# An early job of 272 places, the rest of its expert with the tokens held stationary, and GpSimd's last work shared with VectorE

## The chip, the cores and the metric

The kernel runs on one core of a Trainium2 chip. The metric is the device time of one execution in microseconds (us). Three runs of the kernel before took 909.02, 901.28 and 900.65 us; their median is 901.28 us. The profiled execution, from which every duration below comes, took 895.38 us, and its recorded span is 893.5 us, so 1.9 us lie outside the span and the median lies 5.9 us above it.

## The reference

The inputs are q, k and v with 8 batches, 8 heads, 576 positions and 64 features, and the weights of a mixture of 8 experts. Cut to what matters:

```python
scores = scale * q @ k.T
thresh = scores.max(-1) - tau
attn   = exp(where(scores >= thresh, scores, -1e9) - scores.max(-1))
attn   = attn / (attn.sum(-1) + 1e-9)
x      = (attn @ v)                      # to 4608 tokens x 512
skip   = x @ w_skip > 0                  # only these are computed
e      = argmax(x @ w_gate);  g = its softmax weight
out    = x + g * (relu(x @ w1[e]) @ w2[e])   # 512 -> 1024 -> 512; others pass
```

With the inputs that are drawn, the eight experts get 393, 350, 336, 298, 275, 263, 237 and 197 tokens (worked out from the reference on a host). 357 of the 393 are known before the last five 128-token tiles are through the gate.

## The kernel before, in words

**Precision.** Products of the mixture are made of three products each: a float32 operand is split into a high part that TensorE's fp32r type holds and a low part (the difference), and high·high, low·high and high·low are summed. In the attention the weights `p` are split into float16 parts in the same way, `phh`/`tph` (high, L540 on ScalarE or L542 on VectorE) and `phl`/`tpl` (low, L1009, on GpSimd only); `ph..` is of 128 rows x 1152 and `tp..` the remaining 64 positions of two heads.

**The attention stage.** It is a list of operations, 32 pairs of heads (8 batches x 4). Each pair has scores for the maximum (L824 on TensorE, L829 on VectorE), transposed scores (L797), the exponential (L967, ScalarE), the threshold mask (L972, VectorE, gives `p`), the split, the product with the values (L1037, L1040, L1041, called AV below), and the normalised rows `xb` (L1091) and `x` (L1104) on GpSimd. Rows go to `out` in DRAM; logits come from their transposes (L1147, L1173). For every two batches a gate on VectorE (L1252 to L1411) works out the expert, the gate weight and a place in that expert's list, and GpSimd writes (token, gate) there by indirect DMA, 128 tokens at a time (L1395, `lst<-rec,si`). The last two batches do that in two portions, of four and of five tiles. A planner (class `Plan`, with `SEEDS` for perturbed trials and `OFF` for offsets) simulates the list with a table of costs and so sets the order on every engine.

**The early job.** When all but the last five tiles are in the lists, the expert with most tokens is picked (L1443), and 256 of its tokens become the first job, still inside the plan: the list is loaded, ids are made (L1498, L1499, VectorE), rows are gathered (L529, GpSimd), transposed (L1570), and put through layer 1 (L1603 on TensorE; L1617 and L1620 finish it), whose weights were split on L1541.

**The jobs behind it.** They are in program order: rows are gathered (L1822, issued at L529), transposed and split (`prep_x`, L1832 to L1841), then layer 1 (L1845; products at L1857) and layer 2. Layer 2 either holds blocks of up to 128 tokens of `h` stationary and streams 512 columns of w2 (L1881, products at L1891: 24 for each block), or, where the number of places is no multiple of 128 and at most 320 and the job is not the last, holds w2 stationary, streams the places (L1898, products at L1910: 96) and transposes back. Layer 1 always is 96 products of as many columns as there are places. Weights of the next job are split meanwhile (`split_w`, L1817 ScalarE high, L1818 VectorE or GpSimd low). Jobs: early 256; the rest of that expert, 256; then 384, 352, 320, 288, 288, 256, 256. A loop behind them (L2081) takes tokens beyond these places, one pass for each surplus block, and does not run with these inputs.

## Time and profile before

| what | before |
| --- | --- |
| median of three runs | 901.28 us |
| profiled execution / its span | 895.38 / 893.5 us |
| TensorE busy | 859.5 us (96%) |
| attention stage and early layer 1 | 0 to 640.3 us |
| layer 2 of the early job, then the rest of its expert | 641.9 to 682.2 us |
| seven jobs | 682.2 to 887.8 us |
| last store and end | 887.8 to 893.5 us |

A window's row gives the start and end of a stretch, its length, and for each engine the busy us and, in brackets, the number of instructions; then the mean granted clock of TensorE as a share of 2.4 GHz, the busy share of the DMA engines and GB/s. A timeline's row gives the start, the time that a run of like instructions covers, and in square brackets how long the engine sat idle just before, and what ended that.

### The profile page before, as it was taken

The numbers are of one execution on the slowest core, as the hardware profiler recorded it, in microseconds if no ns is written. First come the engines' busy times: TensorE is split into PE (matmuls) and PEld (weight loads), VectorE is DVE, ScalarE is ACT, GpSimd is POOL, SyncE is SP. The second block draws the span as 40 slices with busy tenths as digits, with TensorE's granted clock in tenths as the row PEclk, the third lists the DMA queues.
The fourth block names the chain that finished last, engine by engine and source line by source line (L and its number), as shares of the span: only waits on it lengthen the run. The fifth ranks groups of instructions, "written<-read, shape, count | busy, mean of one in ns | idle before, by whom it ended". The sixth has DMA issues, their size and how long they took to land. (4 is left out here: it accounts for less than half of the span.)

```text
span 893.5 us, 24884 instructions
## 1 busy us (share of the span) xinstructions
PE 859.5 (96%) x9745; PEld 802.5 (90%) x9745; DVE 682.8 (76%) x1605; ACT 607.5 (68%) x923; POOL 666.6 (75%) x461
## 2 busy tenths in 40 slices
PE   9999999999999999999999999989989999999997
PEld 6888999999999999998889998978879898999986
DVE  6888888988997878999888899894535554476782
ACT  1768988798988798888789878786314452454451
POOL 5576998799789798999899979999336455473463
PEclk9999999999999999999999999999999999999999
DMA  7996778569577767857865864523156635544540
GB/s 174 250 217 164 179 168 235 145 157 254 136 154 203 186 149 200 210 130 188 187 145 136 238 150 97 141 99 120 60 164 232 212 97 184 189 146 162 189 139 19
DMA packets 77422, 147.58 MB, mean 165 GB/s; under 512 B 28178, under 2 KB 28178, under 8 KB 77304
## 3 DMA queue, kind: packets, MB, share of 16 engines
q1 hardware_dynamic: 72616, 136.33, 57.9%
q0 software_dynamic: 4544, 9.65, 3.2%
q8 instruction: 77, 1.26, 0.6%
q14 instruction: 41, 0.34, 0.1%
q10 hardware_dynamic: 144, 0.00, 0.0%
HBM read 68.68 MB, written 15.21 MB: 94 GB/s over the span
## 5 line engine op out<-in xcount | busy, mean ns | idle before, releaser
L1009 POOL TENSOR_TENSOR phl<-p,phh 128x1152 f16<-128x1152 f32 x128 | 305.3, 2394 | 36.3 <-ACT phh L540 14.4
L829 DVE TENSOR_REDUCE mx<-banks 128x1 f32<-128x288 f32 x558 | 230.4, 448 | 27.6 <-PE banks L824 25.4
L972 DVE SCALAR_TENSOR_TENSOR p<-banks,e 128x576 f32<-128x576 f32 x288 | 214.3, 752 | 42.4 <-ACT e L967 38.2
L967 ACT ACTIVATE e<-banks,ntau 128x576 f32<-128x576 f32 x288 | 207.8, 739 | 49.8 <-PE banks L797 37.9
L824 PE MATMUL banks<-QK 128*128 128x288 f32 x1024 | 192.2, 306 | 6.5 <-DMA QK<-hl 4.1
L797 PE MATMUL banks<-QK 128*128 128x288 f32 x1024 | 183.6, 307 | 4.7 <-DVE p L972 2.9
L824 PEld LDWEIGHTS banks<-QK 128*128 128x128 f32 x1024 | 148.8, 188 | 11.5 <-DVE p L972 4.2
L797 PEld LDWEIGHTS banks<-QK 128*128 128x128 f32 x1024 | 145.9, 190 | 10.8 <-DVE p L972 6.3
L540 ACT ACTIVATE phh<-p 128x1152 f16<-128x1152 f32 x117 | 136.1, 1165 | 17.4 <-DVE p L972 10.8
L1037 PE MATMUL banks<-Vh,phh 128*128 128x65 f16 x1280 | 131.0, 195 | 0.4 <-ACT xf L540 0.4
L1041 PE MATMUL banks<-Vh,phl 128*128 128x65 f16 x1280 | 129.1, 194 | 1.1 <-POOL phl L1009 0.9
L1040 PE MATMUL banks<-Vl,phh 128*128 128x64 f16 x1280 | 129.9, 193 | 0.0
L1037 PEld LDWEIGHTS <-phh 128*128 128x128 f16 x1280 | 116.5, 98 | 7.1
L1041 PEld LDWEIGHTS <-phl 128*128 128x128 f16 x1280 | 117.3, 97 | 1.8 <-POOL phl L1009 1.7
L1040 PEld LDWEIGHTS <-phh 128*128 128x128 f16 x1280 | 117.5, 99 | 0.5 <-issue 0.4
L1818 POOL TENSOR_TENSOR wl<-wr,wh 128x1024 fp32r<-128x1024 f32 x28 | 72.5, 2606 | 33.5 <-ACT wh L1817 25.7
L1857 PE MATMUL hps<-xh,wl 128*128 128x256 f32 (+4 forms) x256 | 76.7, 300 | 0.0
L599 POOL TENSOR_TENSOR hl<-raw,hl 128x576 fp32r<-128x576 f32 x43 | 61.6, 1439 | 20.0 <-DVE hl L599 13.0
L1857 PE MATMUL hps<-xh,wh 128*128 128x256 f32 (+4 forms) x248 | 75.9, 306 | 0.0
L1857 PE MATMUL hps<-xl,wh 128*128 128x256 f32 (+4 forms) x248 | 74.8, 302 | 0.0
L1869 POOL DMA_INDIRECT out<-o,ids x21 | 21.1, 1004 | 71.9 <-DVE o L1868 29.2
L1858 ACT ACTIVATE QK<-hps 128x256 fp32r<-128x256 f32 (+4 forms) x64 | 26.9, 421 | 67.8 <-PE hps L1857 67.1
(251 smaller groups left out, 1882.1 us busy)
## 6 DMA issues: line engine op xcount, KB each, us to landing
QK<-hl SPq DMA_DIRECT2D x192, 288.0 KB
wr<-in_w SPq DMA_DIRECT2D x31, 1024.0 KB
raw<-in_qk SPq DMA_DIRECT2D x32, 576.0 KB
vraw<-in_vl SPq DMA_DIRECT2D x32, 320.0 KB
out<-xb SPq DMA_DIRECT2D x32, 256.0 KB
BD<-hl SPq DMA_DIRECT2D x64, 64.0 KB
QK<-QK SPq DMA_DIRECT2D x32, 76.5 KB
out<-x SPq DMA_DIRECT2D x8, 128.0 KB
```

The lines of the kernel that those rows point to most:

```text
L540: nc.scalar.activation(dst, src, AF.Copy)
L797: nc.tensor.matmul(ps[:, j, 0:HS], w_, x_[:, js], start=(i == 0), stop=(i == len(mm) - 1))
L824: nc.tensor.matmul(ps[:, 0:HS], w_, x_[:, js], start=(q == 0), stop=(q == len(mm) - 1))
L829: nc.vector.tensor_reduce(T["mx", g][:, o, j : j + 1], T.pop(("S", g, i, j))[:, 0:HS], AX.X, ALU.max)
L967: nc.scalar.activation(e, T["W", g, i][:, :, 0:HS], AF.Exp, bias=ntau, scale=0.125)
L972: nc.vector.scalar_tensor_tensor(T[z][:, kt % 2].rearrange("p (a b) -> p a b", a=2), T.pop(("W", g, i))[:, :, 0:HS], 0.0, T.pop(("e", g, i ...
L1009: nc.gpsimd.tensor_tensor(T["pl", g, i], T.pop(z)[:, 0:nk], T["ph", g, i], op=ALU.subtract)
L1037: nc.tensor.matmul(pv[:, c, :], x, Vh[:, vh, kt, :], start=(j + q + c == 0), stop=False, skip_group_check=True)
L1040: nc.tensor.matmul(pv[:, c, 0:D], x, Vl[:, vh, kt, :], start=False, stop=False, skip_group_check=True)
L1041: nc.tensor.matmul(pv[:, c, :], y, Vh[:, vh, kt, :], start=False, stop=(c == NM), skip_group_check=True)
L1818: lo[q % 2].tensor_tensor(w[1][:, sl], rs, w[0][:, sl].bitcast(F32), op=ALU.subtract)
L1857: nc.tensor.matmul(hp_[:, 0:cap], w_, x, start=(i == 0), stop=(i == len(mm) - 1))
```

## The change

Constants: the early job has 272 places (`CAPE`) in three blocks of 128, 128 and 16; the rest of its expert is a job `j1` of 128 places (`REST`); the seven jobs have 356, 344, 304, 280, 268, 256 and 204 places. The planner gets another list of 37 seeds (41 before), so the order of the whole attention stage is another one.

For the last two pairs, `shared()` lets the planner put `phl`/`tpl` and `xb`/`x` on VectorE as well as GpSimd.

The last 128 tokens of the picked expert lie partly in the last five tiles. Their ids and gates no longer come from the list: for each of the five tiles VectorE makes a 128x128 selection matrix (`pick_`), TensorE multiplies it with the tile's (gate, token) columns (`sum_`, 2 columns), and the result is added to what the list held before (`recb`, loaded with the early list by two more DMAs). Eight small operations (`q1` to `q5`) make the offsets.

The early job's layer 1 is made one 128-row piece of `h` at a time, all of it behind the last logits; its layer 2 is the transposed form, with the products in an order that takes low weight parts late. Beside it the next expert's w1 is split and `j1`'s rows are prepared. `j1`'s layer 1 (`layer1_s`) holds its tokens stationary and streams 512 columns of w1 (24 products), then transposes `h` back (8 transposes). The lists of the other experts are loaded behind the issue of the next expert's w1.

```diff
-CAPE = 256
-CAPS = (512, 384, 352, 320, 288, 288, 256, 256)
+CAPE = 272
+REST = 128
+CAPS = (0, 356, 344, 304, 280, 268, 256, 204)
...
-XMID = (19, 19, 23, 23)
+XMID = (8, 12, 16, 20)
...
+    def either(e):
+        return nc.gpsimd if e == POOL else nc.vector
+
+    def shared(g, pool, dve):
+        return {POOL: pool, DVE: dve} if g >= NG - LASTS else {POOL: pool}
...
+        lo = pl.op(n + OFF["pl"], fpl, [ph], shared(g, w * 0.00208 + 0.04, w / 960 + 0.1), port=BOTH)
...
+        def pick_(t):
+            if t % 4 == 0:
+                T["sel", t // 4] = ap_.tile([P, 4, P], F32, name="xf", tag="xf", bufs=2)
+            nc.vector.tensor_scalar(
+                T["sel", t // 4][:, t % 4, :], iof, tb, G["slot"][:, t : t + 1], op0=ALU.add, op1=ALU.is_equal
+            )
+
+        def sum_(t):
+            if t == 0:
+                T["rows1"] = g_tile()[:, 0, 0:2]
+            nc.tensor.matmul(
+                T["rows1"], T["sel", t // 4][:, t % 4, :], G["rec"][:, t, 1:3], start=(t == 0), stop=(t == nt - 1)
+            )
+
+        def ids_():
+            nc.vector.tensor_tensor(id1, T["rows1"][:, 1:2], recb[:, 0:1], op=ALU.add)
+
+        def gates_():
+            nc.vector.tensor_tensor(rec1[:, 0, 1:2], T["rows1"][:, 0:1], recb[:, 1:2], op=ALU.add)
...
+            nc.vector.tensor_scalar(b0, b0, float(CAPE), 1.0, op0=ALU.min, op1=ALU.add)
...
+            nc.vector.scalar_tensor_tensor(tb, pks[:, 1:2], float(NTOK), b0, op0=ALU.mult, op1=ALU.add)
...
+            mine = lstv[:, ds(early["ev"], 1), :, :].rearrange("p e c b -> p (e c) b")
+            nc.sync.dma_start(rec0, mine[:, 0:NE, :])
+            c, r = divmod(CAPE, P)
+            nc.sync.dma_start(recb[0 : P - r], mine[r:P, c, :])
+            if r:
+                nc.sync.dma_start(recb[P - r : P], mine[0:r, c + 1, :])
...
-        for f2 in range(NFT // 2):
+        for f in range(NFT):
...
-                        mm_ += [(w_h(d, fs), a), (w_h(d, fs), b_), (w_l(d, fs), a)]
...
+                        T["h0", f] = bank()[:, 0:CAPE]
+                    three = ((w_h, j.xh), (w_h, j.xl), (w_l, j.xh))
...
-                        k2 + 1 + f2 + 0.5 * i,
+                        k2 + 1 + 0.5 * f + 0.1 * i,
...
+    def plan_rest(k, j):
+        acc, ids_, gates_ = T["acc"]
+        T["id1"] = pl.op(k, ids_, acc + [T["rec0"]], {DVE: 0.12})
...
+    def list_(e):
+        nb = jobs[e + 1].nb
+        nc.sync.dma_start(recs[:, e, 0:nb, :], lstv[:, ds(evs[e], 1), 0:nb, :].rearrange("p e c b -> p (e c) b"))
...
+        def run(d, kinds):
+            if d not in yps:
+                yps[d] = ps_y.tile([P, 512], F32, name="yps", tag="yps")
+            for f in range(NFT):
+                for i in kinds:
+                    h, w_ = three[i]
+                    nc.tensor.matmul(
+                        yps[d][:, 0:cap],
+                        w_[:, f, d * P : (d + 1) * P],
+                        h[:, f, 0:cap],
+                        start=(f + i == 0),
+                        stop=(f == NFT - 1 and i == 2),
+                    )
...
+        ready = ((0, (0, 1)), (1, (0, 1)), (0, (2,)), (1, (2,))) if j is j0 else ((0, (0, 1, 2)), (1, (0, 1, 2)))
+        for d, kinds in ready + ((2, (0, 1, 2)), (3, (0, 1, 2))):
+            run(d, kinds)
...
+            for i, (x, w_) in enumerate(mm):
+                nc.tensor.matmul(hp_, x, w_, start=(i == 0), stop=(i == len(mm) - 1))
...
+            nc.scalar.activation(hs[:, fs], hp_, AF.Relu)
+        for q in range(2):
+            tp = ps_h.tile([P, 512], F32, name="hps", tag="hps")
+            for i in range(4):
+                nc.tensor.transpose(tp[:, i * P : (i + 1) * P], hs[:, (4 * q + i) * P : (4 * q + i + 1) * P], ident)
+            tv = tp.rearrange("p (f n) -> p f n", n=P)
+            hh, hl = (a[:, 4 * q : 4 * q + 4, 0 : j.cap] for a in (j.hh, j.hl))
+            nc.scalar.activation(hh, tv, AF.Copy)
...
     w2s, parts = split_w(w2v[ds(early["ev"], 1)], early["raw2"], (nc.vector, nc.vector))
...
+    w1v1 = w1v[ds(evs[1], 1)].rearrange("a p t f -> p (a t) f")
+    w1s, parts = split_w(w1v[ds(evs[1], 1)], [load_w(w1v1, i) for i in range(2)], (nc.vector, nc.vector))
+    list_(1)
+    for e in range(2, E):
+        expert_(e)
+        list_(e)
+    side = {d: [part] for d, part in enumerate(parts)}
+    side[2][:0] = [lambda d=d: prep_x(j1, d) for d in range(NDT)]
+    backs = layer2_t(j0, w2s, side)
+    gather_x(jobs[2])
+    layer1_s(j1, early["w1"], {0: backs})
     mids = {}
     for d, i in enumerate(XMID):
-        mids.setdefault((j0.nb - 1, i), []).append(lambda d=d: prep_x(jobs[1], d))
-    layer2(j0, w2s, {}, mids)
-    parts = []
+        mids.setdefault((0, i), []).append(lambda d=d: prep_x(jobs[2], d))
+    layer2(j1, w2s, {}, mids)
```

How instructions move, at three places. The first is the end of the attention stage on GpSimd. `lst<-rec,si` is a list write, `phl<-p,phh` and `tpl<-p,tph` are low parts, `xg<-out,id` is a gather of the early job's rows. Before:

```order
L1395 DMA lst<-rec,si 36864x2
L1009 TENSOR_TENSOR phl<-p,phh 128x1152
L1395 DMA lst<-rec,si 36864x2 x3
L1009 TENSOR_TENSOR tpl<-p,tph 128x576
L1009 TENSOR_TENSOR phl<-p,phh 128x1152 x2
L529 DMA xg_11841<-out,id_149 128x512 x2
L1009 TENSOR_TENSOR phl<-p,phh 128x1152
L1009 TENSOR_TENSOR tpl<-p,tph 128x576
L1009 TENSOR_TENSOR phl<-p,phh 128x1152 x3
L1091 TENSOR_TENSOR xb<-a,z 128x2x4x64
L1104 TENSOR_TENSOR x_10097<-a,z 64x128
```

With the change:

```order
L1021 TENSOR_TENSOR phl<-p,phh 128x1152
L1021 TENSOR_TENSOR tpl<-p,tph 128x576
L1103 TENSOR_TENSOR xb<-a,z 128x2x4x64
L1116 TENSOR_TENSOR x_10175<-a,z 64x128
L1452 DMA lst<-rec,si 36864x2 x12
L1103 TENSOR_TENSOR xb<-a,z 128x2x4x64
L1452 DMA lst<-rec,si 36864x2
L1021 TENSOR_TENSOR phl<-p,phh 128x1152
L1021 TENSOR_TENSOR tpl<-p,tph 128x576
L1636 TENSOR_TENSOR wl_12001<-wr,wh_11936 128x512
L535 DMA xg_12026<-out,id_149 128x512 x2
L535 DMA xg_12027<-out,id_149 16x512
```

Twelve list writes in one run and a thirteenth now stand ahead of the last `phl` on GpSimd and of the early gathers; where four `phl` stood behind the gathers, none does, and a weight split (L1636) stands ahead of them.

The second is VectorE at the same place (`p<-banks,e` is a mask, `id<-rec` makes the early ids, `wl<-` is a low part of the early w1). Before:

```order
L1541 TENSOR_TENSOR wl_11714<-raw_11453,wh_11532 128x512 x2
L972 SCALAR_TENSOR_TENSOR p<-banks,e 128x576 x2
L1083 RECIPROCAL z<-z 128x10
L972 SCALAR_TENSOR_TENSOR p<-banks,e 128x576 x3
L1498 CAST id_149<-rec_148 128x2
L1499 TENSOR_SCALAR id_149<-rec_148 128x2
L1541 TENSOR_TENSOR wl_11714<-raw_11453,w_11723 128x512 x2
L972 SCALAR_TENSOR_TENSOR p<-banks,e 128x576 x6
L1579 TENSOR_TENSOR QK_106<-banks,QK_105 128x512
```

With the change:

```order
L984 SCALAR_TENSOR_TENSOR p<-banks,e 128x576 x2
L1199 TENSOR_TENSOR lg<-lg,banks 128x64
L984 SCALAR_TENSOR_TENSOR p<-banks,e 128x576 x2
L1199 TENSOR_TENSOR lg<-lg,banks 128x64
L984 SCALAR_TENSOR_TENSOR p<-banks,e 128x576
L1589 CAST id_149<-rec_148 128x3
L1590 TENSOR_SCALAR id_149<-rec_148 128x3
L554 CAST wh_11936<-wr 128x512
L1021 TENSOR_TENSOR phl<-p,phh 128x1152
L554 CAST wh_11936<-raw_11848 128x512
L1021 TENSOR_TENSOR phl<-p,phh 128x1152
L1636 TENSOR_TENSOR wl_12001<-wr,wh_11936 128x512 x3
```

Before, six masks follow the early ids; now the ids come behind the last mask, and VectorE makes low parts `phl` there (seven of the eight of the last two pairs, with those that stand earlier).

The third is the head of the mixture, on TensorE: the end of layer 2 of the early job and what follows. Before (`yps` is layer 2, `xtp` a transpose of gathered rows; layer 1 of the rest follows, 96 products of 256 columns):

```order
L1891 MATMUL yps<-wl,QK_105 128x512 x4
L1839 MATMUL xtp<-ident,xg 128x128 x4
L1891 MATMUL yps<-wl,QK_105 128x512 x4
L1839 MATMUL xtp<-ident,xg 128x128 x4
L1857 MATMUL hps<-xh,wh_11532 128x256
```

With the change, behind the early job's 96 products of 272 columns (`hps<-w..,xh` is the stationary form of `j1`'s layer 1):

```order
L2042 MATMUL hps<-wl_12143,xh 128x512
L2042 MATMUL hps<-w_12090,xh 128x512
L2042 MATMUL hps<-w_12090,xl 128x512
L2042 MATMUL hps<-wl_12143,xh 128x512
L2049 MATMUL hps<-ident,hs 128x128 x8
L1985 MATMUL yps<-wh,QK_105 128x512
L1985 MATMUL yps<-wh,QK_106 128x512
```

The 96 products of 256 columns are gone; 24 of 512 columns and 8 transposes stand in their place, and `j1`'s layer 2 has one block of 24 products, with the transposes of the next job's rows among them. On SP's queue there, before:

```order
L1678 TENSOR_LOAD tabp
L1638 ISA
L1638 DMA recs<-lst 128x4
L1678 TENSOR_LOAD tabp
L1638 ISA
L1638 DMA recs<-lst 128x4
L525 ISA
L525 DMA wr<-in_w 128x2x1024
L525 ISA
L525 DMA wr<-in_w 128x2x1024
```

and with the change:

```order
L1774 TENSOR_LOAD tabp
L531 ISA
L531 DMA wr<-in_w 128x2x1024
L531 ISA
L531 DMA wr<-in_w 128x2x1024
L1771 ISA
L1771 DMA recs<-lst 128x6
L1774 TENSOR_LOAD tabp
L1771 ISA
L1771 DMA recs<-lst 128x6
```

The two loads of w1 now stand ahead of the seven list loads.

## Rows read from the trace of the kernel before

**Rows 1.** the page, part 1: busy us (share of span) and instructions of each engine

```profile
PE 859.5 (96%) x9745; PEld 802.5 (90%) x9745; DVE 682.8 (76%) x1605; ACT 607.5 (68%) x923; POOL 666.6 (75%) x461
```

**Rows 2.** windows: stretch, length, busy us (count) by engine, clock, DMA share, GB/s

```profile
0.00:600.00 600.00, 580.90 (x7778) 546.04 (x7778) 516.80 (x1335) 485.65 (x721) 515.06 (x366) 1.00 0.71 175
600.00:622.00 22.00, 18.90 (x294) 17.31 (x293) 13.16 (x22) 15.14 (x23) 20.97 (x13) 0.92 0.35 125
622.00:641.90 19.90, 18.28 (x171) 17.86 (x167) 7.86 (x43) 7.06 (x14) 5.80 (x8) 0.91 0.20 68
641.90:682.20 40.30, 37.34 (x211) 32.00 (x212) 19.67 (x28) 11.97 (x21) 18.71 (x14) 0.96 0.57 184
682.20:887.80 205.60, 204.11 (x1304) 189.28 (x1301) 124.55 (x180) 87.66 (x146) 105.11 (x62) 1.00 0.45 152
```

**Rows 3.** windows of L1857 alone, layer 1: 384 and 256 columns; PE, PEld, clock, DMA

```profile
682.20:699.20 17.00, 16.90 (x96) 16.60 (x96) 1.00 0.47 146
...
865.00:876.90 11.90, 11.79 (x96) 11.61 (x96) 1.00 0.11 41
```

**Rows 4.** windows of L1891 alone, layer 2: 24 products of 512 columns

```profile
699.00:704.70 5.70, 5.65 (x24) 4.34 (x24) 1.00 0.42 115
```

**Rows 5.** timeline of PE: start, length of a run, operation, count, idle before and releaser

```profile
641.91 4.04 PE L1891 MATMUL yps<-wh,QK 128*128 128x512 f32 x16 [1.63 <-ACT wh L1817]
...
655.17 1.45 PE L1839 MATMUL xtp<-ident,xg 128*128 128x128 f32 x4 [2.85 <-DMA xg<-out,ids]
```

**Rows 6.** timeline of PE, first transposes of a job and the layer 1 behind them

```profile
681.71 0.81 PE L1839 MATMUL xtp<-ident,xg 128*128 128x128 f32 x6
682.28 0.42 PE L1857 MATMUL hps<-xh,wh 128*128 128x384 f32 x1
```

**Rows 7.** timeline of PE, a transposed layer 2 that waits

```profile
799.45 0.40 PE L1910 MATMUL yps<-QK,wl 128*128 128x288 f32 x1 [1.21 <-POOL wl L1818]
```

**Rows 8.** timeline of ACT, the last of the early job and the first weights

```profile
640.32 0.60 ACT L1617 ACTIVATE QK<-banks 128x512 fp32r<-128x512 f32 x1 [0.81 <-PE banks L1603]
640.81 3.89 ACT L1817 ACTIVATE wh<-wr 128x1024 fp32r<-128x1024 f32 x4
```

**Rows 9.** timeline of DVE, the same stretch

```profile
640.95 0.69 DVE L1620 SCALAR_TENSOR_TENSOR QK<-banks,QK 128x512 fp32r<-128x512 f32 x1 [0.40 <-ACT QK L1617]
641.89 4.63 DVE L1818 TENSOR_TENSOR wl<-wr,wh 128x1024 fp32r<-128x1024 f32 x4 [0.25 <-ACT wh L1817]
```

**Rows 10.** timeline of POOL, end of the attention stage

```profile
601.22 0.97 POOL L1395 DMA_INDIRECT lst<-rec,si  x1 [0.30 <-issue]
...
608.55 1.23 POOL L529 DMA_INDIRECT xg<-out,id  x1 [0.38 <-DVE id L1499]
...
614.72 7.04 POOL L1009 TENSOR_TENSOR phl<-p,phh 128x1152 f16<-128x1152 f32 x3
```

**Rows 11.** timeline of POOL, the last five list writes

```profile
639.84 1.05 POOL L1395 DMA_INDIRECT lst<-rec,si  x1 [12.40 <-DVE si L1367]
...
644.27 1.97 POOL L1395 DMA_INDIRECT lst<-rec,si  x1 [0.30 <-issue]
646.54 0.97 POOL L1395 DMA_INDIRECT lst<-rec,si  x1 [0.30 <-issue]
```

**Rows 12.** timeline of DVE, first mask of the last pair and the early ids

```profile
602.87 0.76 DVE L972 SCALAR_TENSOR_TENSOR p<-banks,e 128x576 f32<-128x576 f32 x1 [0.15 <-ACT e L967]
...
607.10 1.11 DVE L1498 CAST id<-rec 128x2 int32<-128x2 f32 x1
```

**Rows 13.** windows of the stretches before which TensorE had waited

```profile
603.70:607.10 3.40, 3.40 (x25) 3.07 (x24) 1.44 (x3) 2.31 (x5) 3.40 (x2) 0.50 0.51 161
...
654.90:658.30 3.40, 3.03 (x9) 2.28 (x10) 0.85 (x2) 0.77 (x2) 0.30 (x1) 0.50 0.67 167
```

**Rows 14.** timeline of SP's queue, eight list loads and the next weights

```profile
648.64 6.90 SPq L1638 DMA_DIRECT2D recs<-lst  x8
655.79 1.03 SPq L525 DMA_DIRECT2D wr<-in_w  x2
```

More of the change, by code (lines that the diff above doesn't have):

```diff
@@ L61 @@
 EB = 2
+LASTS = 2
+LPE = 0.13
 PFB = 4
@@ L1379, in plan_gate @@
         w = ex
-        for f in (b1, b2, b3):
+        final = pr == B // 2 - 1 and t0 + nt == NTP
+        for f in (b1, b2, b3) + ((b1b,) if final else ()):
             w = pl.op(k + gs * 8, f, [w], {DVE: 0.12}, port=BOTH)
@@ L1430, in __init__, with x @@
             self.nb = -(-cap // P)
+            self.own = None
         def m(self, t):
             return min(P, self.cap - t * P)
+        def x(self, t):
+            return self.own[t] if self.own else self.xg[0 : self.m(t), t, :]
     j0 = Job(CAPE, rec0, id0[:, 0, :])
-    jobs = [j0] + [
-        Job(CAPS[e] - (CAPE if e == 0 else 0), recs[:, e], ids[:, e]) for e in range(E)
-    ]
+    j1 = Job(REST, rec1, id1)
+    jobs = [j0, j1] + [Job(CAPS[e], recs[:, e], ids[:, e]) for e in range(1, E)]
     def view1(w):
@@ L1504, in plan_early @@
         stored += [T["tails", bb] for bb in range(1, B - 2, 2)]
-        for t in range(CAPE // P):
+        for t in range(NE):
             def ga(t=t):
                 if t == 0:
-                    early["xg"] = cp.tile([P, CAPE // P, DM], F32, name="xg0")
-                gather(early["xg"][:, t, :], id0[:, 1, t : t + 1], NTOK - S - TL)
+                    early["xg"] = cp.tile([P, XT, DM], F32, name="xg0")
+                    last = ep.tile([P, DM], F32, name="xg2")
+                    j.own = [early["xg"][:, i, :] for i in range(XT)] + [last[0 : j.m(XT)]]
+                gather(j.own[t], id0[0 : j.m(t), 1, t : t + 1], NTOK - S - TL)
             gs.append(pl.op(k + 2, ga, [o, *stored] + [(y,) for y in gs[-1:]], {POOL: 1.04}, lat=3.0, port=()))
@@ L1558, in plan_early @@
         j.hh, j.hl = (q[:, 0:nh].rearrange("p (f n) -> p f n", n=CAPE) for q in flat)
[L1559 to L1572 removed]
+        j.xh, j.xl = (q[:, nh : nh + nx].rearrange("p (d n) -> p d n", n=CAPE) for q in flat)
@@ new lines, in plan_early, with xsl, xps @@
+        full, rest = XT * P, CAPE - XT * P
+        def xsl(q, a):
+            return q[:, 2 * a : 2 * a + 2, 0:full] if a < 2 else q[:, :, full:]
+        def xps(a):
+            n = full if a < 2 else rest
+            return T["x0", a][:, 0 : n * (2 if a < 2 else NDT)].rearrange("p (d n) -> p d n", n=n)
+        def xt(a):
+            T["x0", a] = bank()
+            ps = xps(a)
+            if a < 2:
+                for d in range(2):
+                    for t in range(XT):
+                        nc.tensor.transpose(
+                            ps[:, d, t * P : (t + 1) * P], j.own[t][:, (2 * a + d) * P : (2 * a + d + 1) * P], ident
+                        )
+            else:
+                for d in range(NDT):
+                    nc.tensor.transpose(ps[:, d], j.own[XT][:, d * P : (d + 1) * P], ident[0:rest, 0:rest])
@@ L1783, in attn_moe_kernel @@
     plan_sort(T["ke"])
+    plan_rest(T["ke"], j1)
     plan_w2()
@@ L2049, in attn_moe_kernel @@
         backs = []
-        if k >= 2:
-            for f in range(NFT):
-                side.setdefault(f, []).append(lambda: next(table, None))
+        for f in range(NFT):
+            side.setdefault(f, []).append(lambda: next(table, None))
         if not nxt:
```

265 lines of the change are left out of this document (140 added, 125 removed), and 8 rows, old and new, of the table SEEDS.

## The prediction

> **What bounds the kernel now.** I read the shares of busy time first: TensorE is busy 96% of the span, every other engine 76% or less [rows 1]. Then the span in windows, to see where the idle 4% lies [rows 2]: the attention stage to 600 us has TensorE busy 580.9 of 600 us; the seven jobs from 682.2 to 887.8 us have 204.11 of 205.60; the 82 us between hold 7.7 us of idle time and run below full clock (0.92, 0.91, 0.96). So a job is as long as its products, and only the middle has waits worth removing. The clock shows in two short windows [rows 13]: 3.4 us with 0.50 granted, which is 1.2 GHz, behind waits of TensorE (the second behind the 2.85 us wait of [rows 5]). The profiled execution took 895.38 us, 5.9 under the median of 901.28; I make the sum against the former.
>
> **Smaller jobs (682.2 to 887.8 us).** Layer 1 is 96 products. With 384 columns they take 16.90 us, with 256 11.79 [rows 3]: 0.0399 us a column for all 96. The columns removed are 28+8+16+8+20+0+52 = 132, which gives 5.3 us. The transposed layer 2 has 96 products as well, and its three jobs lose 16+8+20 = 44 columns: 1.8. The other four jobs stay at three and two blocks of 24 products of 512 columns, 5.45 us a block (5.65 less the overlap at its ends [rows 4]): nothing. Below 256 columns the line is an extrapolation: a 128-column product cannot be had faster than a transpose of 128 columns steps, about 0.10 us (0.57 us for six [rows 6]); the 204-column job by the line needs 0.101 us a product, so it is near a floor and could lose nothing below 0.12. I take 1 us off for it: **−6.0**. Ends: −8, if the 1.21 us wait for a weight part [rows 7] goes as well; −4.5, if shorter jobs wait more for weights whose splits stay as long.
>
> The Trainium skill, "TensorE: Matmul & The Clock Gate", section on LDWEIGHTS, has a weight load of 128 columns take 1/1.2 ns each, 107 ns whatever streams: by that the 204-column layer 1 would take 10.3 us instead of the line's 9.7, a loss of 0.6. No row of before has fewer than 256 columns.
>
> **The head, from the first weight part (641.91) to the first big job's layer 1 (682.28): 40.4 us** [rows 5, 6]. Before, two blocks of layer 2, a 2.85 us wait for gathered rows with 1.2 GHz behind it, 96 products of 256 columns, and two more blocks. After:
> - the early job's layer 2, transposed, 96 products of 272 columns: 11.79 + 16 × 0.0399 = 12.4; its first 32 products use weights at 0.51 us a part, while ScalarE makes a part in 0.97 (3.89 for four [rows 8]), so it waits about 1.4 and I take 1.9; four transposes 0.4. The low parts, VectorE's 4.63 us [rows 9], are needed 5.5 us in. Sum 14.8.
> - the rest's layer 1 with tokens stationary: 24 products of 512, 5.45; 12 transposes of the early job's results 1.3, 8 of `h` 0.9; then a chain that nothing covers: relu 0.60, transpose, copy 0.60 [rows 8] and difference 0.69 [rows 9], of which half hides behind the other half: 1.3. Sum 8.95.
> - its layer 2: 5.45, and 12 transposes 1.3: 6.75.
>
> That is 30.5, so **−9.9**. The wait for rows is to go because ids come from products, not from lists behind five writes and eight loads (6.90 us of issue [rows 14]); the gather still follows the five writes on GpSimd, which end at 647.5 [rows 11], and has over 5 us until the transposes at about 653. Cost if that cover is gone: 2.85 plus half of 3.4 us at low clock, −5.5; the other end, no waits at all, −12. The next job's rows come late only if the list loads, now behind two weight loads on SP, wait: those issue in 1.03 us [rows 14], and the rows are needed some 15 us later. If the weights' buffers hold SP until the split of w2 ends (646.5 [rows 9]), there are still 10 us. I cost this at nothing.
>
> **The early job's layer 1 and the selection.** 16 columns more, 0.6 us by the line; five selection products of 2 columns and four transposes of 16 rows, about 0.6. VectorE's five selection matrices and its offsets (some 15 small operations of 0.16 to 0.2 us) lie beside those products: VectorE is busy 7.86 of 19.9 us there [rows 2]. **+1.2.**
>
> **The end of the attention stage.** From the last pair's first mask (602.87 [rows 12]) to the last of the early layer 1 (640.3 [rows 8]) it takes 37.4 us. GpSimd is the pace there: 20.97 of 22 us busy [rows 2], three low parts of 2.35 us each behind the early gathers [rows 10], and the last product with the values waits for them. Seven of eight such parts go to VectorE, where a like operation takes 1.16 us for 1024 columns (4.63 for four [rows 9]), so about 1.3. That frees up to 3.8 us. Against it: 13 list writes now bunch ahead of the early gathers, each 0.97 quiet with 0.30 between [rows 10], 16.5 us; the ids come behind the last mask, where before six masks followed them; and all 96 products of layer 1 now stand behind the last logits, where 24 stood ahead. Here a row matters: the same write takes 1.97 us while VectorE subtracts with both inputs in SBUF, 0.97 when that is over [rows 11]. `phl` on VectorE is such a subtraction. If four writes are stretched by 1 us, that is +4, and the gathers and so layer 1 come later by as much. I take **−1**; ends −8 (GpSimd's relief also ends waits further up) and +9.
>
> The Trainium skill, "SBUF — State Buffer", section "Who interferes with whom", holds that a VectorE tensor_tensor of two SBUF inputs disturbs GpSimd's reads and infers that it does not hold up descriptor writes: by that the 13 writes cost only their 1.3 us each, 16.5 in all. The measured 1.97 speaks against it, and the measurement decides: by it the burst takes up to 20.5.
>
> **The attention stage to 600 us.** The new seeds reorder all 32 pairs. Nothing in the trace prices that; TensorE idles 19.1 of 600 us there [rows 2], 0.6 a pair, so the gain is bounded by that, and the loss by nothing shown. I take zero.
>
> **Sum:** −6.0 −9.9 +1.2 −1 = −15.7: profiled 879.7, median 885.6. Forecast **885 us**.
>
> **Rivals.**
> - *Relief pays more.* GpSimd is at 20.97 of 22 us [rows 2]; freed of 16 us of low parts, the tail shortens by the 3.8 above, and nine list writes that no longer stand between low parts give back some more: −8 in place of −1, 878 us. Against: VectorE takes the parts at 1.3 each and is needed for masks. Chance 0.20.
> - *The burst delays the gathers.* 13 writes at up to 2 us ahead of the gathers; TensorE waits ahead of layer 1 and then runs 3.4 us at 1.2 GHz (1.7 lost [rows 13]): +7 in place of −1, 893 us. For it: [rows 11]. It decides if the writes run while VectorE subtracts. Chance 0.18.
> - *The other side: the new order costs a wait in each pair.* Place: the masks and low parts that the products of each pair wait for, from 0 to 600 us. Price: 32 times the wait. From 0.49 us a pair (15.7/32) nothing is left of the gain; from 0.77 ((15.7+9)/32) it is slower by over 1%. TensorE's idle 19.1 us would have to become 35 or more. At 0.8 us a pair 911 us, at half of that 898. Chance 0.08.
> - *Places too few:* a surplus pass would load 4.2 MB of weights (two matrices of 512 x 1024 in float32) that nothing hides, 23 us at the 184 GB/s of the head [rows 2], 908 us. The counts of tokens (350, 336, 298, 275, 263, 237, 197 against the seven places; 393 against 272+128) fit by 5 or more, so 0.02.
>
> **How the numbers follow.** The forecast's own range is 880 to 891 with chance 0.52. The range 872 to 899 takes in the relief, the burst and the ends of the head; what is left out is most of the reorder case, the surplus passes and the far ends, 0.16. 1% (9 us) is about what a measurement here can tell from no change. Faster than 892.3: the forecast nearly whole (0.50), the relief (0.20), under half of the burst case (0.06): 0.76. Slower than 910.3: 0.05. The rest, 0.19, is the same.
>
> **What would show it.** In the profile after: windows of the seven jobs that sum to some 199 us; the time from the first product of the early layer 2 to the first of the 356-column job, 30 to 31 us with no wait over 2 us; list writes of about 1 us in the burst at the end of attention and no wait of over 1 us ahead of the early job's transposes; TensorE busy about 580 of the first 600 us. What would make it wrong: a wait for the gathered rows of the second or the next job, list writes near 2 us, or more idle time in the first 600 us.

## The result and the profile after

The change makes the kernel slower, by 0.6%. In 21 runs it took 908.49 us in the median (898.09 to 912.78), the kernel before 901.87 (894.59 to 909.02): ratio 1.0058, 95% interval 1.0033 to 1.0082. The medians are of all executions, the ratio is of those within 1.5% of the fastest of their kernel. A second comparison (e13) gave 1.0064 (1.0040 to 1.0087). The forecast was 885, the range 872 to 899.

The rows below are from a second profile of the changed kernel (e13, 900.28 us), since the first was of an execution of 912.08 us, among its longest. Page, part 1:

```profile
PE 851.9 (95%) x9736; PEld 794.4 (88%) x9736; DVE 684.3 (76%) x1629; ACT 607.2 (68%) x925; POOL 646.9 (72%) x448
```

TensorE has 7.6 us less to do than in [rows 1], and GpSimd 19.7 less, as intended. The windows are cut at the same marks in every kernel: M, last mask, last product with the values (AV), last of the early layer 1, first product of the first big job (356 columns, 384 before), last product. M is the ninth of the last pair's 18 maxima of scores; the recorded expectations below call it the last maximum, but nine more follow it, over 9.6 to 10.5 us in the order of before and 14.4 us in that of the change. After:

```profile
0.00:579.30 579.30, 560.61 (x7458) 527.20 (x7459) 490.72 (x1260) 467.91 (x691) 487.66 (x345) 0.99 0.74 177
579.30:625.20 45.90, 38.34 (x550) 36.52 (x546) 32.41 (x102) 28.40 (x45) 28.32 (x25) 0.89 0.15 49
625.20:630.40 5.20, 4.50 (x103) 4.13 (x100) 5.16 (x9) 4.53 (x8) 4.25 (x3) 1.00 0.73 241
630.40:653.90 23.50, 19.74 (x153) 18.76 (x151) 13.20 (x57) 6.24 (x15) 3.73 (x3) 0.93 0.35 117
653.90:690.40 36.50, 31.46 (x192) 27.23 (x191) 19.52 (x31) 14.58 (x25) 15.31 (x11) 0.95 0.61 215
690.40:890.60 200.20, 197.19 (x1301) 180.61 (x1299) 122.50 (x174) 85.59 (x144) 106.46 (x62) 1.00 0.46 153
```

The same windows of a second profile of the kernel before (e8, 901.38 us):

```profile
0.00:583.60 583.60, 563.07 (x7477) 529.40 (x7478) 494.34 (x1284) 466.82 (x694) 495.88 (x354) 1.00 0.72 176
583.60:620.60 37.00, 32.10 (x480) 28.89 (x479) 29.52 (x70) 31.07 (x47) 34.31 (x22) 1.00 0.40 134
620.60:628.80 8.20, 8.20 (x161) 8.00 (x160) 2.39 (x5) 3.27 (x6) 8.04 (x6) 1.00 0.01 2
628.80:646.10 17.30, 17.26 (x124) 16.87 (x121) 6.76 (x40) 4.64 (x11) 2.51 (x5) 0.80 0.22 77
646.10:688.50 42.40, 37.54 (x213) 32.42 (x213) 20.64 (x31) 13.60 (x24) 19.98 (x15) 0.96 0.54 176
688.50:893.90 205.40, 203.98 (x1303) 189.16 (x1300) 124.42 (x180) 87.58 (x146) 105.09 (x62) 1.00 0.46 152
```

Executions differ by 8 us ahead of the first mark alone, so I take means: of three profiles with the order of before (the first, e8, e1) and of four of the change (the first, e2, e13, and e6 up to its own edit). The last AV is left out as a mark, since 24 products of layer 1 moved from ahead of it to behind it.

| stretch, us | before | after | difference |
| --- | --- | --- | --- |
| start to M | 582.9 | 580.3 | −2.6 |
| to the last mask | 37.3 | 45.8 | +8.5 |
| to the end of the early layer 1 | 24.0 | 31.1 | +7.1 |
| to the first big job (without e6) | 42.6 | 37.3 | −5.3 |
| the seven jobs (without e1, e6) | 205.5 | 200.7 | −4.8 |

The sum is +2.9; the medians are 5 to 7 apart. Counted from the maximum that is really the last, the first two rows are +1.8 and +4.1 instead of −2.6 and +8.5. Two thirds of the gains came, and the end of the attention stage lost more than that. GpSimd there (timeline, as in [rows 10]), and TensorE's waits:

```profile
595.48 1.50 POOL L1452 DMA_INDIRECT lst<-rec,si  x1 [1.10 <-DVE banks L890]
...
606.58 0.97 POOL L1452 DMA_INDIRECT lst<-rec,si  x1 [0.30 <-issue]
614.35 0.97 POOL L1452 DMA_INDIRECT lst<-rec,si  x1 [6.81 <-DVE pb L1539]
...
626.42 2.24 POOL L535 DMA_INDIRECT xg<-out,id  x1 [0.47 <-DVE id L1590]
```
```profile
599.30 0.19 PE L1052 MATMUL banks<-Vl,phh 128*128 128x64 f16 x1 [0.49 <-issue]
600.07 0.19 PE L1049 MATMUL banks<-Vh,phh 128*128 128x65 f16 x1 [0.54 <-issue]
...
603.03 0.22 PE L1049 MATMUL banks<-Vh,tph 128*128 128x65 f16 x1 [1.16 <-issue]
604.47 0.21 PE L1052 MATMUL banks<-Vl,tph 128*128 128x64 f16 x1 [1.07 <-issue]
605.91 0.23 PE L1049 MATMUL banks<-Vh,tph 128*128 128x65 f16 x1 [1.17 <-issue]
...
633.65 0.98 PE L1672 MATMUL banks<-ident,xg 128*128 128x128 f32 x7 [2.02 <-DMA xg<-out,id]
636.38 0.60 PE L1677 MATMUL banks<-ident,xg 16*128 16x16 f32 x4 [1.75 <-DMA xg<-out,id]
656.60 5.78 PE L2005 MATMUL yps<-QK,wh 128*128 128x272 f32 x32 [1.66 <-DVE pb L1392]
...
685.73 0.30 PE L1933 MATMUL xtp<-ident,xg 100*128 100x100 f32 x1 [1.78 <-DMA xg<-out,ids]
```

Nine list writes in a row run from 595.48 to 607.55. From the third on, and for a little over 1 us behind the last, TensorE stops nine times, 6.9 us in all, for nothing that the profile shows (only stops of 0.3 us or more are counted here and below). In the first profile of before, where writes came in runs of at most five, there is no such stop. Then TensorE idles 2.02 and 1.75 us for the early job's rows: their gather starts 47 us behind M, where before it started 30 behind. The clock falls behind each of these places (windows of the half-speed stretches, 0.50 granted, as in [rows 13]); in the first profile and in e6 the second of them lasts 13.7 us:

```profile
602.20:612.40 10.20, 5.65 (x70) 5.12 (x71) 1.64 (x4) 1.53 (x4) 4.25 (x4) 0.50 0.02 2
636.30:639.70 3.40, 3.33 (x18) 2.98 (x19) 0.23 (x1) 0.84 (x3) 0.00 (x0) 0.50 0.94 358
656.80:660.20 3.40, 3.40 (x17) 3.40 (x17) 3.40 (x4) 1.36 (x2) 3.40 (x1) 0.50 0.19 15
```

### The profile page after: what moved, and what is told of

Same layout as the page of the kernel before. It is cut to its first block, busy times and chain, and to the rows that moved or that the text cites. A ratio compares the mean times of both kernels' runs of the same rounds, so it can differ in the third digit from the quotient of the medians.

```text
span 910.3 us, 24881 instructions
## 1 busy us (share of the span) xinstructions
PE 858.1 (94%) x9736; PEld 798.6 (88%) x9736; DVE 686.0 (75%) x1629; ACT 607.7 (67%) x925; POOL 646.2 (71%) x448
## 5 line engine op out<-in xcount | busy, mean ns | idle before, releaser
L1021 POOL TENSOR_TENSOR phl<-p,phh 128x1152 f16<-128x1152 f32 x121 | 288.7, 2395 | 67.4 <-ACT phh L552 39.0
L841 DVE TENSOR_REDUCE mx<-banks 128x1 f32<-128x288 f32 x558 | 227.6, 449 | 29.8 <-PE banks L836 28.2
L1049 PEld LDWEIGHTS <-phh 128*128 128x128 f16 x1280 | 117.7, 99 | 7.6 <-issue 0.6
L1052 PEld LDWEIGHTS <-phh 128*128 128x128 f16 x1280 | 118.7, 99 | 1.7 <-issue 1.5
L1911 POOL TENSOR_TENSOR wl<-wr,wh 128x1024 fp32r<-128x1024 f32 x26 | 67.7, 2619 | 23.0 <-ACT wh L1910 15.4
L1452 POOL DMA_INDIRECT lst<-rec,si x36 | 42.7, 1186 | 37.0 <-DVE xf L1377 21.4
L1911 DVE TENSOR_TENSOR wl<-wr,wh 128x1024 fp32r<-128x1024 f32 x34 | 60.7, 1800 | 9.7 <-ACT wh L1910 8.9
L1951 PE MATMUL hps<-xh,wh 128*128 128x356 f32 (+6 forms) x224 | 67.5, 301 | 0.4 <-DVE QK L1953 0.4
L1951 PE MATMUL hps<-xl,wh 128*128 128x356 f32 (+6 forms) x224 | 66.5, 297 | 0.0
L1951 PE MATMUL hps<-xh,wl 128*128 128x356 f32 (+6 forms) x224 | 66.4, 296 | 0.0
```

The lines of the kernel that those rows point to most:

```text
L841: nc.vector.tensor_reduce(T["mx", g][:, o, j : j + 1], T.pop(("S", g, i, j))[:, 0:HS], AX.X, ALU.max)
L1021: either(e).tensor_tensor(T["pl", g, i], T.pop(z)[:, 0:nk], T["ph", g, i], op=ALU.subtract)
L1049: nc.tensor.matmul(pv[:, c, :], x, Vh[:, vh, kt, :], start=(j + q + c == 0), stop=False, skip_group_check=True)
L1052: nc.tensor.matmul(pv[:, c, 0:D], x, Vl[:, vh, kt, :], start=False, stop=False, skip_group_check=True)
L1911: lo[q % 2].tensor_tensor(w[1][:, sl], rs, w[0][:, sl].bitcast(F32), op=ALU.subtract)
L1951: nc.tensor.matmul(hp_[:, 0:cap], w_, x, start=(i == 0), stop=(i == len(mm) - 1))
```

## Experiments

The kernels of one group ran on one chip beside the kernel before, each group on another: e1 to e4; e5 to e8; e9 to e12; e13 to e16; e17 and e18. Kernels that were run in two groups show how far a ratio can differ between them: the fillers 0.9972 and 1.0020, a mixed version 0.9948 and 0.9993, with intervals that overlap. Differences of 0.005 across groups settle nothing.

**e1: the smaller jobs alone,** in the kernel before.

```
-CAPS = (512, 384, 352, 320, 288, 288, 256, 256)
+CAPS = (512, 356, 344, 304, 280, 268, 256, 204)
```

> The kernel before, with only the places of the seven jobs changed to 356, 344, 304, 280, 268, 256 and 204. Theory (the term of -6.0 in the prediction): layer 1 and the transposed layer 2 shorten by their columns; the seven jobs take 199 to 200 us instead of 205.6 and the kernel is 4.5 to 7 us faster (ratio 0.992 to 0.995). Rival (the jobs wait for their weights instead): the products shorten but waits for low parts of weights (1.2 us before) grow to 3 us or more, and the kernel gains less than 3 us.

902.65 us, ratio 1.0016 (0.9984 to 1.0048). The seven jobs take 202.4 us for 205.5, a gain of 3.1 that the total doesn't show. One transposed layer 2 waits more than in [rows 7], and the next one, which before waited 0.15 us at most, waits 2.41:

```profile
802.92 0.40 PE L1910 MATMUL yps<-QK,wl 128*128 128x280 f32 x1 [1.50 <-POOL wl L1818]
833.37 0.39 PE L1910 MATMUL yps<-QK,wl 128*128 128x268 f32 x1 [2.41 <-POOL wl L1818]
```

These waits are 3.9 us together, as the rival has it. So jobs alone pay little: shorter jobs run into their weights.

**e2, e8, e13: change, before, and change again, nothing edited.**

> The changed kernel once more, for a second trace of it. Theory 1 (TensorE's stops of 0.4 to 1.2 us with no releaser between 606 and 617 us belong to the run of nine list writes on GpSimd at 602.7 to 614.8): they are there again, 6 to 8 us in sum, at the same products. Rival (they were an accident of one execution): none or elsewhere.

> The kernel before once more, for a second trace. The first profiled execution took 895.38 us, 6 under its median. If the prediction's base was a lucky execution, the difference lies in the attention stage: the last product with the values at 628 to 633 us instead of 624.6, with some stretch of it at half clock, and the later stages as long as before (42 us from the early layer 1 to the first big job, 205.5 for the seven jobs). If the jobs vary too, their sum differs by over 1 us.

> The changed kernel itself, unchanged, on the same chip as the next three. Theory A (TensorE's stops without a releaser belong to the kernel, nine list writes in a row): they are there again, 5 to 7 us between 595 and 617 us, last maximum to last mask 45 to 46 us, ratio to before 1.003 to 1.008. Rival B (they belong to some chips or executions, since three kernels with the same nine writes showed none on another chip): none here or in the next ones, and then the nine writes cost by GpSimd's time alone, 40 to 43 us, and the ratio is 0.999 to 1.003.

The stops come back in e2 (12 stops, 6.8 us) and e13 (the nine above); e8 has a single one, of 0.33 us. On the chip of e9 to e12, three kernels with the same nine writes had none; theory A of e13 holds on its chip, and its rival on that one.

**e3: the nine writes left out** of the change.

```
             def sca(t=t):
+                if pr == 2:
+                    return
```

> The changed kernel without the nine list writes of the third pair of batches (their tokens are missing from the lists, and pass unchanged; places, products and the order of everything else stay). Theory 1 (the run of writes stops TensorE): no stops without releaser behind 606 us, no half clock there, the last product with the values 8 to 11 us earlier than 637, and the kernel 6 to 10 us faster than the changed one (895 to 902). Rival (the stops come from elsewhere, and the writes cost GpSimd time alone): the stops stay, and the kernel gains at most 3 us.

894.98 us, ratio 0.9925 (0.9895 to 0.9955), 1.3% below the change by the ratios. No stops there; M to last mask 37.2 us.

**e4: the change in the order of the kernel before.** The planner's search is replaced by a table of that order; the new operations stand beside the old ones that they replace.

```
-        span = self.forward(lambda i, e: ops[i].key + ops[i].off.get(e, 0.0), not seeds)
...
+        p = [x / 100.0 for x in WHEN]
+        return self.forward(lambda i, e: p[i], True)
```

> The changed kernel with the order of the kernel before: each operation that both have stands in the planner's list at the time and on the engine that the kernel before gave it, new ones are put in beside their like; so nothing is shared between GpSimd and VectorE. Theory A (the new order of the attention stage is what costs: it falls 12 us behind up to the last product with the values and 12 more up to the end of layer 1): the last product with the values comes at 624 to 629 us, the early layer 1 ends at 643 to 648, and the kernel takes 885 to 893 us, 1 to 2% under the kernel before. Rival B (the new parts of the tail cost it: three gathers, the selection, 272 places, all of layer 1 behind the logits): layer 1 still ends at 655 or later and the kernel takes 900 us or more.

900.42 us, ratio 0.9994 (0.9964 to 1.0025): not the 885 to 893 of theory A, but close to its rival (layer 1 ends at 653.6). M to the last mask takes 37.7 us as before, with two stops, of 0.36 and 0.33 us; from there to the end of layer 1 it takes 28.3, for 24.0 before and 31.1 in the change. So the order is one part of the loss, and the new parts of the tail are another.

**e5 and e7: the writes spread out,** by putting the end of the third gate 40 us earlier on VectorE and its writes one by one between low parts on GpSimd (a table, as in e4); e7 has e6's edit too.

> The changed kernel with one thing moved: the end of the gate of the third pair of batches stands 40 us earlier on VectorE, and its nine list writes stand one by one among GpSimd's low parts (546 to 578 us in the planner's time, where 583 to 592 was one run). All writes are made. Theory 1 (a long run of writes stops TensorE): no stops without releaser and no half clock at 600 to 620 us; the last product with the values comes 5 to 9 us earlier than in the changed kernel's runs (629.7 and 637.3 us), and the kernel takes 895 to 900 us. Rival (the time goes to GpSimd, whose writes then delay its low parts where the products with the values wait for them; leaving the writes out gained because of their 11.5 us alone): 903 us or more.

> Both edits, the spread writes and the early rows. If both theories hold they add up: 891 to 896 us, 0.6 to 1.1% under the kernel before. If the writes only move the loss to GpSimd: 899 us or more.

e5: 908.40, ratio 1.0068 (1.0041 to 1.0094). e7: 909.46, 1.0069 (1.0041 to 1.0096). The stops are gone, and TensorE waits for GpSimd instead; the half-speed stretch behind it stays:

```profile
598.24 0.24 PE L1366 MATMUL banks<-Vh,phl 128*128 128x65 f16 x1 [3.46 <-POOL phl L1334]
```

**e6: ids and gathers of the 356-job issued inside the early job's layer 2.**

```
+    side[2].append(lambda: gather_x(jobs[2]))
     backs = layer2_t(j0, w2s, side)
-    gather_x(jobs[2])
```

> The changed kernel with the ids and the gather of the 356-place job issued inside the early job's layer 2, ahead of the last weight part on VectorE, where it stood behind it and behind the loads of w2. Theory (the head gave only 5 of the 10 us because the rows of the next job come late: waits of 1.6 and 0.9 us and 3.4 us at half clock behind them): these waits go, the stationary layer 1 to the next job's first product takes 16 us instead of 20, and the kernel is 3 to 5 us faster than the changed one (903 to 905). Rival (the rows wait for the lists, not for VectorE): under 1 us.

902.14 us, ratio 1.0002 (0.9983 to 1.0022). The wait for the next job's rows (1.78 us above) is gone, the stretch to the first big job falls from 37.3 to 35.9. It falls by no more because another wait stands in it, for the rows of the rest of the expert:

```profile
670.19 0.41 PE L1933 MATMUL xtp<-ident,xg 128*128 128x128 f32 x2 [1.92 <-DMA xg<-out,id]
```

Those 1.4 us are what the rows show; against the change's ratio it would be 5, but the totals of e5 and e7, of one group, differ by nothing. The size stays open.

**e9 and e14: filler products ahead of the early job's transposes,** 16 and 18 of 0.115 us.

```
+            t.more = (16, 0, 18)[a]
```

> The changed kernel with 16 filler products ahead of the early job's transposes and 18 ahead of the third block's, so that TensorE does not stand idle in its two waits for gathered rows (the waits themselves stay). Theory A (the tail is long because TensorE idles for rows and then runs at 1.2 GHz, 13.7 us of it behind 640 us in the profile of the change): the half-clock stretch behind the last product with the values goes or shrinks to 3.4 us, the time from that product to the last of the early job's layer 1 falls from 26.7 us to 20 to 23, the kernel is 3 to 6 us faster than the change: ratio to the kernel before 0.999 to 1.003. Rival B (the wait for rows and the 96 products behind it cost what they do at any clock): 25 to 27 us, ratio 1.004 to 1.008.

> The changed kernel with the 16 and 18 filler products again, beside the unchanged one. Theory A (low clock behind waits for rows is a cost of its own): 3 to 6 us faster than the change on the same chip (0.994 to 0.997 of it), no half-clock stretch behind the last product with the values. Rival B (the gain of the earlier run came from the chip): within 2 us of the change.

e9: 895.69, ratio 0.9972 (0.9931 to 1.0012); e14: 905.30, 1.0020 (0.9989 to 1.0051), beside 905.68 of the change. No half-speed stretch is left between the last AV and the end of the early layer 1, which lies 22.8 and 22.4 us behind it, for 23.5 in e13. The medians of e13 and e14 differ by 0.4, the ratios by 4 us with overlapping intervals: a gain of 0.4 to 4 us, not settled.

e9's profile has twelve writes in a row, the nine among them, and no stops. TensorE waited 4.2 us for GpSimd's normalised rows behind them; e10 3.94, e12 3.0.

**e10: the early job's rows loaded early,** from fixed places.

```
-                gather(j.own[t], id0[0 : j.m(t), 1, t : t + 1], NTOK - S - TL)
+                nc.sync.dma_start(j.own[t], out[t * P : t * P + j.m(t), :])
```

> The changed kernel in its own order, but the early job takes the first 272 rows of the output array by plain loads on SP, issued some 12 us before its gathers would be (wrong tokens, so the gathering of the early job is left out). Theory A (most of the 11 us that the stretch from the last product with the values to the end of the early layer 1 has grown by is the wait for rows behind GpSimd's gathers): 26.7 falls to 16 to 19 us, kernel 7 to 9 us faster than the change, ratio 0.996 to 0.999. Rival B (the 96 products behind the last logits are the cost, the rows are there anyway): at least 24 us, ratio 1.004 to 1.008.

898.61, ratio 0.9981 (0.9935 to 1.0026). The early layer 1 ends 18.4 us behind the last AV, as theory A has it: of the change's 25.9 us (four profiles) some 7 are the wait for rows and the clock behind it. The ratio leaves out the rival's 1.004 to 1.008, but its chip is the one without stops, so the total says little of the rows.

**e11 and e15: the nine writes replaced by memsets** of like length on GpSimd.

```
                 if pr == 2:
+                    for _ in range(8):
+                        nc.gpsimd.memset(idle9, 0.0)
+                    return
```

> The changed kernel with each of the nine list writes of the third pair of batches replaced by eight small memsets on GpSimd of 0.1 us each (those tokens reach no list, as in the run without the nine): GpSimd is held about as long, but no indirect DMA is made. Theory A (it is the nine indirect writes in a row that stop TensorE): no stops without a releaser in the last pairs, last maximum to last mask 37 to 40 us, ratio 0.992 to 0.997. Rival B (nine writes cost by the 11 us in which GpSimd makes no low parts): 43 to 46 us, ratio 1.002 to 1.007.

> The nine writes of the third pair of batches replaced by 72 memsets of 0.16 us again (those tokens reach no list), beside the unchanged change. Theory A (indirect writes stop TensorE): no stops where the change has them, last maximum to last mask 38 to 39 us as in the earlier run, 7 to 11 us faster than the change. Rival B (GpSimd's 12 us alone are the cost): within 3 us of the change, and no stops in either.

e11: 891.13, ratio 0.9931 (0.9896 to 0.9967). e15: 893.42, 0.9907 (0.9871 to 0.9943), beside the change's 1.0064 on the same chip. e15, GpSimd and TensorE:

```profile
594.72 11.64 POOL L1454 MEMSET idle<- 128x8 f32 x72
```
```profile
611.95 1.12 PE L1159 MATMUL banks<-ident,xb 128*128 128x128 f32 x4 [2.97 <-POOL xb L1103]
```

GpSimd is held 11.64 us as by the writes, and nothing stops TensorE but one wait of 2.97 for it; M to last mask takes 38.5 us, for 46.0 in e13. So it is the indirect writes, not GpSimd's time, that cost most of the 8.5: 38.5 and 38.6 with memsets, 40.2 to 43.0 (e9, e10, e12) with writes where TensorE doesn't stop, 45.3 to 47.3 where it does. The nine fall between M and the last pair's first mask, and there it shows most plainly: 24.2 us before, 25.1 with memsets, 25.1 to 26.7 with writes and no stops, 35.4 to 37.0 with stops. The totals differ by 12 us, more than these 7; e15's profile is of its longest run, so where the rest lies is not shown.

**e12 and e16: a mixed version:** e6's and e9's edits, and the third block's transposes behind the last logits; the nine writes stay.

> A version meant to beat both: the change in its own order with the ids and gathers of the 356-token job issued in the early job's layer 2, 16 filler products ahead of the early job's transposes, and the third block's transposes behind the last logits. The burst of nine writes stays. If the two waits for rows and the half clock behind them are what the tail and the head lose, 895 to 899 us, ratio 0.993 to 0.998; if the burst's stops decide alone, as the run with early rows alone: 900 to 904, ratio 0.998 to 1.002.

> The version meant to beat both on another chip, beside both. If the earlier result holds: ratio to before 0.992 to 0.998, 895 to 899 us where before takes 901; if it was that chip: 0.998 to 1.002. Last product with the values to the end of the early layer 1: 20 to 22 us, and 35 to 36 from there to the first big job.

893.63, ratio 0.9948 (0.9916 to 0.9981), and on the second chip, where the stops are there (10, 6.4 us), 899.91, 0.9993 (0.9965 to 1.0021).

**e17 and e18: the order of before with e6's edit;** e18 adds 18 filler products.

> The change with the order of the kernel before (no run of nine list writes: runs of at most three) and with the ids and gathers of the 356-token job issued in the early job's layer 2. The two repairs have been run apart: the order gave 0.9994, the early rows about 5 us. If they add up and the burst is the rest of the cost: no stops without a releaser over 0.5 us, last product with the values to the end of the early layer 1 17 to 19 us, from there to the first big job 35 to 36, ratio to before 0.993 to 0.998, 894 to 899 us. If early rows gain only what the stops had made late: 0.998 to 1.002.

> The same with 18 filler products ahead of the third block's transposes, where the order of before leaves a wait of 1.8 us and 3.4 us of 1.2 GHz behind it. If the low clock is a cost of its own (half of 3.4 us): 1 to 2 us faster than the run without fillers and no half-clock stretch between 655 and 690 us; if not, the same within 1 us, which these rounds can't tell from nothing.

e17: 891.75 us, ratio 0.9917 (0.9883 to 0.9951). This version beats the kernel before, and by the ratios also the change. Windows from its M on:

```profile
585.00:622.60 37.60, 32.72 (x479) 28.75 (x479) 32.57 (x76) 30.68 (x46) 34.71 (x23) 1.00 0.39 133
622.60:632.60 10.00, 10.00 (x174) 9.45 (x174) 3.24 (x8) 3.67 (x8) 9.51 (x6) 1.00 0.01 2
632.60:648.80 16.20, 16.20 (x125) 15.93 (x123) 7.41 (x44) 5.34 (x12) 1.84 (x3) 0.89 0.25 82
648.80:684.90 36.10, 31.68 (x193) 27.58 (x192) 20.17 (x33) 14.65 (x25) 14.14 (x12) 0.95 0.62 218
684.90:885.00 200.10, 197.12 (x1301) 180.62 (x1299) 122.41 (x174) 85.55 (x144) 106.34 (x62) 1.00 0.45 153
```

No stops. From M to the end of the early layer 1 it takes 63.8 us, for 61.3 before and 76.9 in the change; the stretch to the first big job is 6.5 and the jobs are 5.4 shorter than before. e18: 895.51, 0.9974 (0.9949 to 0.9998). I had put the fillers at the wrong place: the 2.0 us wait is at the transposes of the rest of the expert, not at the early job's third block, and is still there; 18 products without a wait to fill are 2.1 us of work.

## Why the prediction was wrong

**The end of the attention stage (−1, ends −8 and +9) is the step that failed, together with the zero for the new order ahead of it.** From M to the end of the early layer 1 it measured +8.5 +7.1 = +15.6. The prediction counted this stage from the last pair's first mask: from there it takes 41.0 us for 37.2, +3.8 and within the ends, but that mask comes at 616.2 for 607.1, +9.1, where "I take zero" stood. The nine writes lie ahead of that mask, so the burst was priced behind the place where it cost. The parts:
- The relief: up to 3.8 us for VectorE's low parts are not shown. The last mask to the last AV is 3.2 us shorter, but 24 products that left it are 2.8 of that.
- "If four writes are stretched by 1 us, that is +4" had the wrong mechanism. In the burst seven of nine writes took 0.97 us, as in [rows 10]. That 13 writes bunch was right, who pays was not: TensorE does, by stops that no row of before shows, so that [rows 10, 11] gave no price for them.
- "And so layer 1 come later by as much" was under-priced: the gathers start 17 us later against M (13 against the true last maximum), not 4. They stand behind 13 writes and the last pair's low parts, and TensorE has no scores left to cover them: 2.02 and 1.75 us of waits, half speed, and all 96 products of layer 1 behind. With rows that are there early (e10) some 7 us of this go.

So the rival "the burst delays the gathers", 893 us with 0.18, came nearest: its late gathers and half speed are there, its slow writes are not, and the price was twice as high. My sum with the measured terms (−2.6 +15.6 −5.3 −4.8; the +1.2 lies within these) is +2.9, 904 as a median, for 905.68 and 908.49.

The Trainium skill, "SBUF — State Buffer", section "Who interferes with whom", infers that a VectorE tensor_tensor of two SBUF inputs doesn't hold up descriptor writes. The runs went further against it than the 1.97 us of [rows 11]: a write that began 0.16 to 0.22 us behind the first of four such subtractions outlasted all four in ten profiles of the change and of edits of it (5.24 to 5.31 us); in e9, e11 and e12, where it began 1.19 us behind it, it took 2.02.

```profile
656.55 5.29 POOL L1452 DMA_INDIRECT lst<-rec,si  x1 [0.30 <-issue]
```
```profile
656.38 4.61 DVE L1911 TENSOR_TENSOR wl<-wr,wh 128x1024 fp32r<-128x1024 f32 x4
```

**The head (−9.9; measured −5.3).** From the first product of the early layer 2 to the big job it takes 33.8 us in e13 (656.60 to 690.4), forecast 30.5. The transposed layer 2 took 15.4 for 14.8 (whose parts add up to 14.7), in part by luck: the waits of 1.9 us for high parts of weights did not come, and 3.4 us at half speed did. Layer 1 with tokens stationary took 8.6 for 8.95. The rest's layer 2 with its transposes took 9.8 for 6.75: "I cost this at nothing" failed, for the ids of the next job stand on VectorE behind a weight part (674.53), the gathers follow at 674.97, and TensorE waits 1.78 us at 685.73. Ahead of it all TensorE waits 1.66 us for VectorE to finish the ids and gates of the last tokens, which I hadn't costed. The wait for the rest's rows was to go: in e13 it did, in e6 and e17 it is 1.92 and 2.01 us. With the next job's rows early (e17) the head is 36.1 us from the end of the early layer 1.

**The jobs (−6.0; measured −4.8, alone −3.1)** fell within the ends. The seven layers 1 were sized well: 95.9 us in e13 for 100.1 in e8. The three transposed layers 2 gave 0.9 of their 1.8 us, for the waits for weight parts grew: 1.49 and 0.87 in e13, a single 1.22 in e8, and in e1 the 1.50 and 2.41 above. Windows of layer 1 alone in e13 (268 and 204 columns), and two rows from inside the 268-column one:

```profile
815.50:843.80 28.30, 13.24 (x97) 12.25 (x97) 1.00 0.50 166
868.70:890.60 21.90, 10.95 (x96) 10.79 (x96) 1.00 0.10 36
```
```profile
817.09 0.60 PE L2025 MATMUL xtp<-ident,yt 128*128 128x128 f32 x4
826.40 0.39 PE L1951 MATMUL hps<-xh,wh 128*128 128x268 f32 x1 [0.37 <-DVE QK L1953]
```

From its first product to its last the 268-column layer 1 takes 14.16 us, hardly less than the 288 columns before it (14.21). That is not the products, which start every 0.125 us for 0.131: both stretches hold 12 transposes of the job before, 1.4 us, and the shorter one loses 0.5 us around a wait for VectorE. The 204-column one takes 10.95, 0.114 us a product: above the line, and the 1 us that I took off for it was about right (9.7 by the line).

The Trainium skill, "TensorE: Matmul & The Clock Gate", section on LDWEIGHTS, gives 10.3 us there as an estimate, at 107 ns a weight load; the trace lies above it, and nearer to it than to the line.

**Attention up to M (0)** was right within the 8 us by which executions differ: 580.3 for 582.9, so the rival of a wait in each pair did not happen. TensorE is busy 580.3 of the first 600 us in e13, as the prediction's sign asked. The zero failed behind M, as said above. **Places too few** did not happen either: no surplus pass ran.

**The base.** The profiled execution of 895.38 us that I started from was shorter than all but one of the 21 runs; adding 5.9 for the median put that right.

## What to carry to other kernels

When one engine's indirect writes bunch, price them by what stands behind them and by whether the bound engine still has work of its own: in the order of before, in runs of at most five, such writes showed no price that I could find; bunched ahead of a gather they belong to a stage that took some 16 us longer. Spreading them is no cure by itself (e5). A gain that an order's search finds in its model must be looked for at the one place where two queues meet; here the old order with one gather moved kept the gains of the change and lost most of its costs. And compare executions by stages over several profiles: here a single pair would have shown before and after as equal.

## What the runs showed of the hardware

- TensorE stops with no releaser while GpSimd makes nine indirect writes in a row: in e13 instructions start at 599.30, 600.07, 600.80, then at 603.03, 604.47, 605.91, a beat of 0.75 and then 1.44 us, beside writes that start every 1.27. It showed in six profiles on at least three chips (9 to 12 stops, 5.9 to 6.9 us in all), in none of three with the same writes on another, in none with the writes left out, spread or replaced by memsets. Short stops, of 0.3 to 0.6 us and at most two in a row, also stand beside or just behind runs of two or three writes, in some profiles (in e13 at 377.55, 378.33 and 465.63; in e1, of the order of before, at 580.75). What passes between the two engines stays open.
- VectorE took up TensorE's last selection product 1.16 to 1.25 us after its end in ten profiles, and within 0.04 us in e9 to e12, e4, e17 and e18. It doesn't go with the stops: e3, e5, e7 and e15 have the delay and no stops at the end of attention. The ten are those in which the list write beside the weight split took 5.24 to 5.31 us. What causes it stays open. In e13:

```profile
656.17 0.16 DVE L1389 TENSOR_TENSOR id<-banks,pb 128x1 int32<-128x1 f32 x1 [1.21 <-PE banks L1384]
```
